# Attention backward: Z one iteration later, and eight blocks of E transposed in later iterations

## The chip, the cores and the metric

The kernel runs on one core of a Trainium2 chip. The metric is the device time of one execution in microseconds. A profiled execution gives, beside its time, a trace of all instructions: TensorE (PE, with its weight loads as PEld), VectorE (DVE), ScalarE (ACT), GpSimd (POOL) and SyncE (SP), which issues DMAs here.

## The reference

The reference is a layer with its gradients, in bfloat16: a layer norm, attention with 32 heads of width 16 over 2048 positions, multiplied by a gate that comes from a two-layer MLP, and a residual. What is asked for is the output and the gradients for the input and six weights. The part that this case is about is attention with its backward pass:

```
xn = layernorm(x)                       # x: 2048 x 512
q, k, v = split(xn @ wqkv)              # 32 heads of 16
p = softmax(q k^T * 16**-0.5)           # 2048 x 2048 for each head
s = (p v) @ wo
out = x + s * silu(mlp(xn))
# and the gradients of all this for x, wqkv, wo, w1, b1, w2, b2, given grad_out
```

For a head with probabilities p and the gradient dO of its output, the kernel needs sums over keys (the output O = p v, the row sums, and dQ) and sums over queries (dK and dV).

## The kernel before

The program has three stretches: a preparation (projections, the MLP's forward pass), the attention loop, and the remaining gradients. The loop is `attention_core`, and the change touches nothing else.

The loop works on pairs of heads (16 of them) and on quarters of the queries (512, `qc`), which makes 64 blocks `j`. In a block it steps over 16 units, `kb`, of 128 keys each. So there are 1024 units, and a unit's number `g` is also the number of the iteration that holds its main part. "Iteration 4" below means g % 16 = 4. "Key block 1" is the unit with kb = 1.

What is done for a unit:
- `emit_s` (L1115): two matmuls, one per head, give the scores s of 128 keys by 512 queries, in one PSUM tile of a pool with a single buffer. `emit_exp` (L1124, ACT) takes the exponential of both, E, into a ring of 11 SBUF tiles (`ets`).
- `emit_d` (L1137): two matmuls for d = v dO, each into one of three PSUM tiles. `emit_mult` (L1155, DVE) multiplies each with E; the product is G (`gts`). POOL copies one slot of E beside it (L1153).
- `emit_x` (L1232, L1235, L1239): three times four matmuls, which gather in PSUM tile X the sums over keys, from E, from E with ones, and from G. X is copied to SBUF by DVE (`emit_xs`, L1248) once a block, transposed by PE in two halves (`emit_XT`, L1266), copied back (`emit_xt`, L1274), and made into O, dQ and the weights W1 and W2 for Z by POOL (`emit_fin`).
- `emit_dmat` (L1172): a transposing DMA on SP's queue turns two units' G into `gk`.
- `emit_T` (L1192): PE transposes seven of the eight 128 by 128 pieces of E into the PSUM tile tT, of which there is one; the eighth piece is what POOL copied, and goes through the DMA. `emit_cT` (L1208, ACT) copies the result to the SBUF tile `ek`.

Z (`emit_z`, L1334) gathers the sums over queries in a PSUM tile, also single: four matmuls in each iteration, with W1 or W2 as weights and `gk` or `ek` as data. Eight iterations make one Z; then `emit_acc` (L1346 for the first quarter of queries, L1348 for the others, DVE) adds it to an SBUF sum. Z runs `ZOFF` iterations behind the units: at -20 the sums fall into iterations 11 and 3.

In units 0 and 5 the last 256 of the 512 columns of tT are needed for a transposed half of X (`FIN_AT`). For that, `cut` leaves out three of the seven transposes of these units, and ACT's copy is shorter by as much. The pieces left out are transposed later: the tile tT has room for eight pieces, and `OLDER` says in which unit the eighth place takes which older piece; (5, 1) is piece 1 of unit 5. DVE copies that place to `ek` (`emit_cO`, L1215), two iterations after the unit. Blocks from the second on do this; the first transposes all seven at once.

The order of the work is that of the emitted program: each engine goes through its own instructions in order and waits at each for what it needs. In an iteration g, PE's order is: first d of unit g, the two s of unit g+1, second d of unit g, four matmuls for Z, twelve for X of unit g-1, transposes of unit g-1 (and of X in iterations 1 and 6). In iteration 1 the G part of X is left out, and it is made up for in iteration 2, which has sixteen. DVE's order is: copy of the eighth place of unit g-2 if there is one, copy of a transposed half of X if there is one, first product of unit g, copy of X or sum of Z if there is one, second product. ACT's order is: exp of unit g+1, copy of T of unit g-1.

After the last unit the loop goes on for as many iterations as Z runs behind, in which `tail_mid` already starts the output projection (L584, with products by DVE at L586 and L591).

Of the kernel before, what the change touches and what calls it, by code (L numbers as in the profile page):

```python
# [1050 lines left out]
def attention_core(ctx, ctx_r, tc, k, grads, Oall, dQall, dKVT_out, ident_f32, ident_bf, npairs=16, nqc=4):  # L1051
# [67 lines left out]
    def emit_exp(g):  # L1119

        a = a_unit(g)
        if a is None:
            return
        nc.scalar.activation(out=st_et[g].rearrange("k b h q -> k h b q"),  # L1124
                             in_=cur["s"][:].rearrange("k h (b q) -> k h b q", b=4), func=ACT.Exp)
# [15 lines left out]
    def emit_mult(g):  # L1141
        a = a_unit(g)
        if a is None:
            emit_xs(g - 1)
            emit_acc(g + ZOFF)
            return
# [7 lines left out]
        for hj in range(2):  # L1154
# [3 lines left out]
            if hj == 0:  # L1158
                emit_xs(g - 1)
                emit_acc(g + ZOFF)  # L1160

# [9 lines left out]
            gk = blk[j]["Gk"][kc][:, kb % 4 - 1:kb % 4 + 1]  # L1171
            nc.sync.dma_start_transpose(out=gk.rearrange("q r x k -> q (r x) k"), in_=st_gt[g][:].rearrange("k a x q -> k (a x q)"))  # L1172

    OLDER = {4: (0, 0), 6: (0, 1), 7: (0, 2), 8: (5, 0), 12: (5, 1), 13: (5, 2)}

    def cut(g):
        return 3 if g >= 16 and g % 16 in (0, 5) else 0

    def older(g):
        return OLDER.get(g % 16) if 16 <= g < NSTEP else None  # L1180

    def emit_T(g):
        a = a_unit(g)
        if a is None:
            return
        kk = a[1] % 4
        et = st_et[g]
        t = ps_t.tile([128, 512], f32, name="tT")
        tb = t[:].bitcast(bf16).rearrange("q (i k) -> q i k", k=128)
        for i in range(cut(g), 7):  # L1190
            b = i + a[1] // 4 % 2
            nc.tensor.transpose(tb[:, i - cut(g), :], et[:, b // 2, b % 2, :], ident_bf[:])  # L1192
        if older(g):
            kk2, i = older(g)
            b = i + kk2 // 4 % 2
            nc.tensor.transpose(tb[:, 7, :], st_et[g // 16 * 16 + kk2][:, b // 2, b % 2, :], ident_bf[:])
        st_T[g] = t
        if kk == 0:
            cur["ek"] = ekc.tile([128, 4, 7, 128], bf16, name="ek")
            blk[a[0]]["Ek"][a[1] // 4] = cur["ek"]  # L1200

    def emit_cT(g):
        a = a_unit(g)
        if a is None:
            return
        j, kb = a
        c = cut(g)
        nc.scalar.copy(out=blk[j]["Ek"][kb // 4][:, kb % 4, c:7].rearrange("q i k -> q (i k)").bitcast(f32),  # L1208
                       in_=st_T[g][:, 0:(7 - c) * 64])
# [7 lines left out]
    def emit_x(g, part):  # L1217
        a = a_unit(g)
        if a is None:
            return  # L1220
        j, kb = a
        if part == "e" and kb == 0:
            blk[j]["X"] = ps_x.tile([128, 512], f32, name="X", tag="X")
        X = blk[j]["X"]
        NATt = op_of(j)["NAT"]
        et = st_et[g]
        for c in range(4):
            half, hj = c // 2, c % 2
            r = 32 * c
            ev = et[:, half::2, hj, :]  # L1230
            if part == "e":
                nc.tensor.matmul(X[r:r + 32, 0:256], lhsT=NATt[:, kb, hj, 1:33], rhs=ev,  # L1232
                                 start=(kb == 0), stop=False, skip_group_check=True, tile_position=(0, r))
            elif part == "l":
                nc.tensor.matmul(X[r:r + 32, 256:512], lhsT=Lc[:], rhs=ev,  # L1235
                                 start=False, stop=False, skip_group_check=True, tile_position=(0, r))
            else:
                gv = st_gt[g][:, kb % 2, 4 * hj + half:4 * hj + 4:2, :]
                nc.tensor.matmul(X[r:r + 17, 256:512], lhsT=NATt[:, kb, hj, 0:17], rhs=gv,  # L1239
                                 start=False, stop=(kb == 15), skip_group_check=True, tile_position=(0, r))  # L1240

    def emit_xs(g):
        a = a_unit(g)
        if a is None or a[1] != 15:
            return
        j = a[0]
        xs = xsp.tile([128, 512], f32, name="xs", tag="xs")
        nc.vector.tensor_copy(out=xs[:], in_=blk[j].pop("X")[:])  # L1248
        blk[j]["xs"] = xs
# [66 lines left out]
    def emit_z(g):  # L1316
        u = z_unit(g)
        if u is None:
            return
        j, kp, qb, part = u  # L1320
        if part == 0 and qb == 0:
            blk[j]["Z"] = ps_z.tile([128, 512], f32, name="Z", tag="z")
        Z = blk[j]["Z"]
        for par in range(2):
            kc = 2 * kp + par
            for hj in range(2):
                r = 64 * par + 32 * hj
                if part == 0:
                    mv = blk[j]["Gk"][kc][:, :, 4 * hj + qb, :]
                elif 2 * qb + hj == 7 * (1 - par):  # L1330
                    mv = blk[j]["Gk"][kc][:, :, 8, :]
                else:
                    mv = blk[j]["Ek"][kc][:, :, 2 * qb + hj - par, :]
                nc.tensor.matmul(Z[r:r + 32, :], lhsT=WT[j % 2][1 - part][:, qb, hj, :], rhs=mv,  # L1334
                                 start=(part == 0 and qb == 0), stop=(part == 1 and qb == 0), tile_position=(0, r))

    def emit_acc(g):
        u = z_unit(g)
        if u is None or u[2] != 0 or u[3] != 1:
            return  # L1340
        j, kp = u[0], u[1]
        p, qc = blocks[j]
        Z = blk[j]["Z"]
        av = acc[:, kp, :]
        if qc == 0:
            nc.vector.tensor_copy(out=av, in_=Z[:])  # L1346
        else:
            nc.vector.tensor_tensor(out=av, in0=Z[:], in1=av, op=ALU.add)  # L1348
        if qc == nqc - 1:
            ob = (outp.tile([128, 512], bf16, name="ob") if kp == 0 or j < NB - 1 else  # L1350
                  xsp.tile([128, 512], bf16, name="ob", tag="xs"))
            nc.gpsimd.tensor_copy(out=ob[:], in_=av)
            dv = dKVT_out[p * 64:(p + 1) * 64, :].rearrange("r (a b s) -> r a b s", a=2, b=2)
            for b in range(2):
                nc.gpsimd.dma_start(out=dv[:, kp, b, :], in_=ob[b * 64:(b + 1) * 64, :])

    FIN_AT = {1: 1, 6: 0}
    FIN_END = {1: 1, 2: 0}
    ZOFF = -20
    late = []  # L1360
    for hj in range(2):
        emit_s(0, hj)
    emit_exp(0)
    for g in range(NSTEP - ZOFF):
        cur["g"] = g
# [20 lines left out]
        emit_exp(g + 1)  # L1386
        emit_z(g + ZOFF)
        emit_x(g - 1, "e")
# [28 lines left out]
def full_kernel(ctx, tc, A_x, A_wqkv, A_wo, B_x, B_w1, B_b1, B_w2, B_b2, grad_out,  # L1417
# [35 lines left out]
    with ExitStack() as cO, tc.manual_schedule():  # L1453
        op0p = cO.enter_context(tc.tile_pool(name="op0", bufs=1, side="right", reuse_waits="tile"))
        k.op0 = make_op(nc, op0p, 0)
        k.Lc = op0p.tile([128, 32], bf16, name="Lc")
        nc.gpsimd.memset(k.Lc[:], 0.0)
        nc.gpsimd.memset(k.Lc[:, 17:18], 1.0)
        op0p.tile([128, 96], mybir.dt.uint8, name="pad_to_256r")
        kv, nat, q, do, natd = op_loads(k, k.op0, 0, nc.sync.dma_start)  # L1460
        first = dict(kv=kv, q=lambda: (nat(), q()), do=lambda g: (do(g * 512, g * 512 + 512), natd(g * 4, g * 4 + 4)))
        with ExitStack() as cP:
            Pre(cP, tc, k, first, A_x, A_wqkv, A_wo, B_w1, B_b1, B_w2, B_b2, grad_out)
        pO = cO.enter_context(tc.tile_pool(name="persistO", bufs=1, reuse_waits="tile"))
        k.Oall = pO.tile([128, NT, D], bf16, name="Oall", tag="Oall")
        k.dQall = pO.tile([128, NT, D], bf16, name="dQall", tag="dQall")
        grads = Grads(cO, tc, k, pO, op0p, A_x, grad_out, A_wqkv, A_wo, B_w1, B_w2,
                      (out_0, out_1, out_2, out_3, out_4, out_5, out_6, out_7))
        with ExitStack() as cB:
            attention_core(cB, cB.enter_context(ExitStack()), tc, k, grads, k.Oall, k.dQall, k.dKVT_s, k.ident_f, k.ident_bf)  # L1470
        grads.run()
# [56 lines left out]
```

## Time and profile before

| | |
|---|---|
| time, median of 3 runs | 2180.5 us (2179.21 to 2181.51) |
| profiled execution | 2180.46 us |
| its span, first to last instruction | 2178.8 us |
| granted TensorE clock, mean | 0.997 |
| first to last exp of the loop, start to start | 218.7 to 1837.4 us of the span |

The page gives busy times by engine over the whole span and groups of equal instructions, with the mean duration of one and the idle time of its engine ahead of them. Busy times of PE are those of pipelined matmuls, whose ends are modelled, so PE is at 98% without being at its peak. In the timeline each row is a run of equal instructions of one engine: start, duration of the run, engine, line, operation, names, shapes, count, and in brackets the idle time ahead of it with what ended it.

### The profile page before, as it was taken

Reading aid. Unit: us, or ns where it says so; the run is one execution under the profiler, and the core shown is the slowest. Engines: PE = TensorE matmul, PEld = TensorE weight load, DVE = VectorE, ACT = ScalarE, POOL = GpSimd, SP = SyncE. Lnnn points to the kernel's source line nnn. Section 1 sums busy time; section 2 is a strip of 40 time slices with the busy share of each in tenths; the row PEclk is TensorE's granted clock in tenths of the full one; section 3 lists DMA queues with packets and bytes.
Section 4 is the critical chain, followed back from the end, with each engine's and each line's share of the span. In section 5 each row is a group of like instructions: output and inputs, shape, how many; then the busy total and the mean of one; then the engine's idle time right before and its main releaser. Section 6 shows DMA issues by size and latency. Waiting matters only on the chain.

```text
span 2178.8 us, 74934 instructions
## 1 busy us (share of the span) xinstructions
PE 2133.0 (98%) x30659; PEld 1170.6 (54%) x30659; DVE 1898.0 (87%) x3523; ACT 1782.2 (82%) x2481; POOL 870.6 (40%) x2397
## 2 busy tenths in 40 slices
PE   6999999999999999999999999999999999899999
PEld 3444555555555555555555555555555555444444
DVE  6677899999999999999999999999999998788647
ACT  5664899999999999999999999999999997775224
POOL 4376434343434444343434344444434343511003
PEclk9999999999999999999999999999999999999999
DMA  7786999999999999999999999999999999999975
GB/s 235 248 281 202 205 199 198 209 195 200 208 204 198 209 201 201 202 200 206 203 199 201 202 203 201 204 203 204 200 202 206 194 213 212 294 251 240 246 209 178
DMA packets 1416569, 461.17 MB, mean 212 GB/s; under 512 B 1329118, under 2 KB 1400414, under 8 KB 1416224
## 3 DMA queue, kind: packets, MB, share of 16 engines
q1 hardware_dynamic: 1401920, 425.44, 100.3%
q0 software_dynamic: 12720, 29.37, 4.9%
q8 instruction: 240, 3.93, 0.8%
q10 hardware_dynamic: 1584, 1.57, 0.2%
q14 instruction: 105, 0.86, 0.1%
HBM read 62.79 MB, written 64.75 MB: 59 GB/s over the span
## 4 chain that ended last, share of the span: by engine, by line
PE 94%; DVE 2%; DMA 1%; ACT 1%; POOL 0%; issue 0%; SPq 0%; DVEq 0%; ACTq 0%; POOLq 0%
PE tT L1192 22%; PE Z L1334 15%; PE d L1137 15%; PE X L1239 6%; PE X L1232 5%; PE X L1235 5%; PE s L1115 3%; PE ps_dy L909 2%; PE ps_dw L742 2%; PE ps_dw L983 2%; PE ps_h L352 2%; PE ps_m L367 2%; PE ps_dh L875 2%; PE tT L1266 1%; PE ps_dxa L1027 1%; PE ps_dwkv L827 1%
## 5 line engine op out<-in xcount | busy, mean ns | idle before, releaser
L1155 DVE TENSOR_TENSOR gts<-d,ets 128x512 bf16<-128x512 f32 x2048 | 1302.2, 682 | 18.2 <-PE d L1137 3.9
L1124 ACT ACTIVATE ets<-s 128x1024 bf16<-128x1024 f32 x1024 | 1051.6, 1027 | 15.2 <-PE d L1137 3.9
L1208 ACT COPY ek<-tT 128x448 f32<-128x448 f32 (+1 forms) x1024 | 525.1, 513 | 115.0 <-PE tT L1192 31.3
L1192 PE MATMUL tT<-ident_bf,ets 128*128 128x128 bf16 x6790 | 557.9, 221 | 0.0
L1192 PEld LDWEIGHTS <-ets 128*128 128x128 bf16 x6790 | 382.5, 98 | 210.5 <-issue 195.2
L1137 PE MATMUL d<-QDT,KVT 32*128 32x512 bf16 x2048 | 469.4, 384 | 0.0
L1153 POOL COPY gts<-ets 128x128 bf16<-128x128 bf16 x1024 | 281.6, 297 | 387.5 <-ACT ets L1124 382.7
L1115 PE MATMUL s<-QDT,KVT 32*128 32x512 bf16 x2048 | 401.1, 379 | 2.4 <-ACT ets L1124 2.4
L1334 PE MATMUL Z<-gk,W 128*32 128x512 bf16 x2304 | 302.9, 389 | 1.4 <-DVE acc L1348 1.3
L1239 PE MATMUL X<-gts,NAT 128*17 128x256 bf16 x4096 | 290.6, 273 | 0.0
L1232 PE MATMUL X<-ets,NAT 128*32 128x256 bf16 x4096 | 290.4, 273 | 0.0
L1235 PE MATMUL X<-ets,Lc 128*32 128x256 bf16 x4096 | 290.3, 273 | 0.0
L1334 PEld LDWEIGHTS <-W 128*32 128x32 bf16 x4096 | 105.5, 93 | 238.2 <-issue 225.0
L1137 PEld LDWEIGHTS <-KVT 32*128 32x128 bf16 x2048 | 148.5, 91 | 114.3 <-issue 21.5
L1334 PE MATMUL Z<-ek,W 128*32 128x512 bf16 x1792 | 203.6, 389 | 0.0
L1235 PEld LDWEIGHTS <-Lc 128*32 128x32 bf16 x4096 | 110.1, 97 | 108.6
L1215 DVE COPY ek<-tT 128x64 f32<-128x64 f32 x378 | 84.9, 225 | 89.5 <-ACT ek L1208 76.0
L1404 POOL COPY tick<-gts 1x2 bf16<-1x2 bf16 x205 | 36.0, 175 | 313.5 <-DVE gts L1155 313.5
L1115 PEld LDWEIGHTS <-KVT 32*128 32x128 bf16 x2048 | 142.7, 91 | 12.3 <-issue 6.4
L1239 PEld LDWEIGHTS <-NAT 128*17 128x17 bf16 x4096 | 114.7, 91 | 15.4 <-issue 1.1
L1232 PEld LDWEIGHTS <-NAT 128*32 128x32 bf16 x4096 | 108.8, 96 | 5.1 <-issue 5.1
L1295 POOL TENSOR_TENSOR W<-NATQq,rL 128x128 bf16<-128x128 bf16 x64 | 25.5, 399 | 147.9 <-DVE rL L1294 110.3
(252 smaller groups left out, 2470.4 us busy)
## 6 DMA issues: line engine op xcount, KB each, us to landing
gk<-gts SPq DMA_TRANSPOSE x512, 5.6
H1T_s<-h1r SPq DMA_DIRECT2D x28, 256.0 KB, 4.2
HGT_s<-hgT SPq DMA_DIRECT2D x8, 896.0 KB, 4.5
DH_s<-stg SPq DMA_DIRECT2D x12, 512.0 KB, 3.3
hch<-DH_s SPq DMA_DIRECT2D x12, 512.0 KB, 4.8
gp<-H1T_s SPq DMA_DIRECT2D x9, 512.0 KB, 6.8
out_dram<-ob_w POOLq DMA_DIRECT2D x36, 128.0 KB, 4.6
NAT_s<-NS SPq DMA_DIRECT2D x4, 1056.0 KB, 6.1
```

Source lines behind the costliest of these rows:

```text
L1115: nc.tensor.matmul(s[:, hj, :], lhsT=op["KVT"][r:r + 32, kb * 128:(kb + 1) * 128], rhs=op["QDT"][r:r + 32, qc * 512:(qc + 1) * 512], start ...
L1124: nc.scalar.activation(out=st_et[g].rearrange("k b h q -> k h b q"), in_=cur["s"][:].rearrange("k h (b q) -> k h b q", b=4), func=ACT.Exp)
L1137: nc.tensor.matmul(d[:], lhsT=op["KVT"][r:r + 32, kb * 128:(kb + 1) * 128], rhs=op["QDT"][r:r + 32, qc * 512:(qc + 1) * 512], start=True, ...
L1153: nc.gpsimd.tensor_copy(out=gts[:, kb % 2, 8, :], in_=st_et[g][:, b // 2, b % 2, :])
L1155: nc.vector.tensor_tensor(out=gts[:, kb % 2, 4 * hj:4 * hj + 4, :], in0=st_d.pop((g, hj))[:].rearrange("k (b q) -> k b q", b=4), in1=st_et ...
L1192: nc.tensor.transpose(tb[:, i - cut(g), :], et[:, b // 2, b % 2, :], ident_bf[:])
L1208: nc.scalar.copy(out=blk[j]["Ek"][kb // 4][:, kb % 4, c:7].rearrange("q i k -> q (i k)").bitcast(f32), in_=st_T[g][:, 0:(7 - c) * 64])
L1215: nc.vector.tensor_copy(out=blk[g // 16]["Ek"][kk // 4][:, kk % 4, i].bitcast(f32), in_=st_T[g][:, 448:512])
L1232: nc.tensor.matmul(X[r:r + 32, 0:256], lhsT=NATt[:, kb, hj, 1:33], rhs=ev, start=(kb == 0), stop=False, skip_group_check=True, tile_positi ...
L1235: nc.tensor.matmul(X[r:r + 32, 256:512], lhsT=Lc[:], rhs=ev, start=False, stop=False, skip_group_check=True, tile_position=(0, r))
L1239: nc.tensor.matmul(X[r:r + 17, 256:512], lhsT=NATt[:, kb, hj, 0:17], rhs=gv, start=False, stop=(kb == 15), skip_group_check=True, tile_pos ...
L1334: nc.tensor.matmul(Z[r:r + 32, :], lhsT=WT[j % 2][1 - part][:, qb, hj, :], rhs=mv, start=(part == 0 and qb == 0), stop=(part == 1 and qb = ...
```

## The change

Two things are changed. `ZOFF` goes from -20 to -21: every matmul of Z and every sum is emitted one iteration later, the sums so in iterations 12 and 4, and the loop has one iteration more at its end. And `cut` now also leaves out the first two of the seven transposes of unit 1; ACT's copy of this unit gets 320 columns instead of 448. `OLDER` has eight entries instead of six: units 8 and 9 take pieces (1, 0) and (1, 1), unit 11 takes (5, 0), which unit 8 took before.

```
-    OLDER = {4: (0, 0), 6: (0, 1), 7: (0, 2), 8: (5, 0), 12: (5, 1), 13: (5, 2)}
+    OLDER = {4: (0, 0), 6: (0, 1), 7: (0, 2), 8: (1, 0), 9: (1, 1), 11: (5, 0), 12: (5, 1), 13: (5, 2)}

     def cut(g):
-        return 3 if g >= 16 and g % 16 in (0, 5) else 0
+        return {0: 3, 1: 2, 5: 3}.get(g % 16, 0) if g >= 16 else 0
...
     FIN_AT = {1: 1, 6: 0}
     FIN_END = {1: 1, 2: 0}
-    ZOFF = -20
+    ZOFF = -21
```

## The prediction

> **What bounds the kernel now.** I read the page's engine table first, then the groups of instructions with shapes kept apart, then the busy time of one block, then the timeline of that block row by row. A block is 16 iterations of the attention loop; there are 64 of them. I took the block that starts at 751.49 us, because the first rows (PE d L1137) of its iterations lie at the same distances as in most other blocks.
>
> ```profile
> PE 2133.0 (98%) x30659; PEld 1170.6 (54%) x30659; DVE 1898.0 (87%) x3523; ACT 1782.2 (82%) x2481; POOL 870.6 (40%) x2397
> ```
>
> ```profile
> L1155 DVE TENSOR_TENSOR gts<-d,ets 128x512 bf16<-128x512 f32 x2048 | 1302.2, 682 | 18.2 <-PE d L1137 3.9 <-ACT ets L1124 1.1 <-POOL tick L1404 1.0
> L1208 ACT COPY ek<-tT 128x448 f32<-128x448 f32 x898 | 478.2, 533 | 104.5 <-PE tT L1192 31.3 <-PE tT L1196 0.5
> L1215 DVE COPY ek<-tT 128x64 f32<-128x64 f32 x378 | 84.9, 225 | 89.5 <-ACT ek L1208 76.0
> L1208 ACT COPY ek<-tT 128x256 f32<-128x256 f32 x126 | 46.9, 372 | 10.5
> ```
>
> ```profile
> 751.49:776.71 25.22, 25.22 (x438) 14.40 (x437) 23.63 (x45) 23.32 (x33) 12.00 (x37) 1.00 1.26 208
> ```
>
> In this order the last row gives PE, PEld, DVE, ACT and POOL: in 25.22 us DVE is busy 23.63 and ACT 23.32, and the granted clock is 1.00. No engine has much to spare, so what counts is which of them ends last in each iteration. The timeline of iterations 2 to 6 shows it (start us, duration us; mergers of equal instructions have a count):
>
> ```profile
> 754.03 0.40 PE L1192 MATMUL tT<-ident_bf,ets 128*128 128x128 bf16 x4
> ...
> 755.18 1.02 ACT L1124 ACTIVATE ets<-s 128x1024 bf16<-128x1024 f32 x1
> ...
> 755.68 1.87 DVE L1155 TENSOR_TENSOR gts<-d,ets 128x512 bf16<-128x512 f32 x3
> 755.80 0.56 PE L1192 MATMUL tT<-ident_bf,ets 128*128 128x128 bf16 x7
> 756.30 0.39 PE L1137 MATMUL d<-QDT,KVT 32*128 32x512 bf16 x1
> ...
> 756.40 0.53 ACT L1208 COPY ek<-tT 128x448 f32<-128x448 f32 x1 [0.19 <-PE tT L1192]
> 756.41 0.37 PE L1137 MATMUL d<-QDT,KVT 32*128 32x512 bf16 x1
> 756.83 1.03 ACT L1124 ACTIVATE ets<-s 128x1024 bf16<-128x1024 f32 x1
> ...
> 757.47 0.68 DVE L1348 TENSOR_TENSOR acc<-Z,acc 128x512 f32<-128x512 f32 x1
> 757.87 0.38 PE L1137 MATMUL d<-QDT,KVT 32*128 32x512 bf16 x1
> 757.91 0.39 PE L1115 MATMUL s<-QDT,KVT 32*128 32x512 bf16 x2
> ...
> 757.97 0.53 ACT L1208 COPY ek<-tT 128x448 f32<-128x448 f32 x1
> 758.07 3.22 DVE L1155 TENSOR_TENSOR gts<-d,ets 128x512 bf16<-128x512 f32 x5
> 758.40 1.03 ACT L1124 ACTIVATE ets<-s 128x1024 bf16<-128x1024 f32 x1
> 758.68 0.40 PE L1239 MATMUL X<-gts,NAT 128*17 128x256 bf16 x4
> ...
> 759.51 0.38 PE L1137 MATMUL d<-QDT,KVT 32*128 32x512 bf16 x1
> 759.51 0.39 PE L1115 MATMUL s<-QDT,KVT 32*128 32x512 bf16 x2
> ...
> 760.28 0.28 PE L1239 MATMUL X<-gts,NAT 128*17 128x256 bf16 x4
> ...
> 761.05 0.39 PE L1137 MATMUL d<-QDT,KVT 32*128 32x512 bf16 x1
> ...
> 761.60 1.02 ACT L1124 ACTIVATE ets<-s 128x1024 bf16<-128x1024 f32 x1
> ```
>
> Iterations 3 to 6 begin at 756.30, 757.87, 759.51 and 761.05 with their first d. Four gates can be read off.
> (1) s has one PSUM tile, so it starts 0.05 after the exp before it ends (756.83 + 1.03 = 757.86, s at 757.91).
> (2) On ACT the copy of T stands between two exps: it starts 0.10 after PE's next d (757.87, 757.97), and the next exp 0.43 later (758.40), or 0.47 after s, whichever is last.
> (3) d has three tiles: the second d of iteration 3 waits for the first product of iteration 2. That began at 755.68, ended 0.68 later at 756.36, and d follows at 756.41 instead of beside the first d.
> (4) X's last group needs the second product of the unit before. With the sum of Z (757.47) in between, that product starts at 758.07 and ends at 758.75; the group of four, which elsewhere takes 0.28, takes 0.40: a stall of 0.12.
> One transpose costs PE (0.56 - 0.40) / 3 = 0.053, some 0.055 with rounding. From s to PE's next d it is 1.54 with eight transposes (759.51 to 761.05), so 1.48 with seven. On DVE a product or a sum sets back the next by 0.60 (757.47 to 758.07), 0.08 less than its 0.68; so a copy of 0.225 sets it back by 0.14.
>
> **The change, part by part.** PE has the same number of transposes: two leave unit 1 (iteration 2), an eighth appears for units 9 and 11 (iterations 10 and 12); unit 8 keeps its eighth, now another one. ACT's copy of unit 1 shrinks from 448 to 320 columns: between 372 and 533 ns, by columns 533 - 161 x 128/192 = 426, so 0.11 less. DVE gets 2 x 63 = 126 copies like L1215, in iterations 11 and 13. The sums go from iterations 3 and 11 to 4 and 12, every Z one iteration later. No DMA, POOL or SP instruction of the loop is moved past another; POOL's weights for Z get an iteration more.
>
> *Iterations 2 and 3.* T of unit 1 is 0.11 shorter, so the next d comes at 756.19. It gains PE nothing: gate 3 is DVE's, behind X's transposed copy, and its start at 755.68 does not depend on T. The second d stays at 756.41, and all PE work behind it, iteration 4 included (757.87), stays too. ACT gains: exp of unit 3 ends at 756.20, s at 756.25, exp of unit 4 at 756.72 instead of 756.83.
>
> *Iteration 4.* Without the sum, the second product of unit 3 starts at 757.47 and ends at 758.15, so the stall of 0.12 is gone; with s at 757.88 the next d comes at 757.88 + 1.48 = 759.36 instead of 759.51. But exp of unit 5 hangs on the copy at 757.97 and stays at 758.40.
>
> *Iteration 5.* s waits for that exp: 758.40 + 1.03 + 0.05 = 759.48, 0.03 earlier than now. DVE's first product of unit 4 can start at about 758.36 (0.38 for d and some 0.1 to start, as exp starts 0.08 behind an s of 0.39), the sum at 758.96, the second product at 759.56, ending at 760.24. X wants it at 759.48 + 0.77 = 760.25 (0.77 is 759.51 to 760.28) and needs 760.24 + 0.05: a stall of 0.04. The next d comes at 759.48 + 1.54 + 0.04 = 761.06, against 761.05. Exp of unit 7 then stands at 761.06 + 0.53 = 761.59, against 761.60. Both gains have been given back; about -0.01 to -0.02 goes on through iterations 6 to 9, which keep their instructions.
>
> *Iterations 10 to 13*, the same block:
>
> ```profile
> 768.88 0.38 PE L1137 MATMUL d<-QDT,KVT 32*128 32x512 bf16 x1
> 768.98 0.39 PE L1115 MATMUL s<-QDT,KVT 32*128 32x512 bf16 x2
> ...
> 768.99 0.53 ACT L1208 COPY ek<-tT 128x448 f32<-128x448 f32 x1
> 769.45 1.02 ACT L1124 ACTIVATE ets<-s 128x1024 bf16<-128x1024 f32 x1
> ...
> 770.01 0.68 DVE L1346 COPY acc<-Z 128x512 f32<-128x512 f32 x1
> 770.46 0.38 PE L1137 MATMUL d<-QDT,KVT 32*128 32x512 bf16 x1
> 770.53 0.39 PE L1115 MATMUL s<-QDT,KVT 32*128 32x512 bf16 x2
> ...
> 771.30 0.34 PE L1239 MATMUL X<-gts,NAT 128*17 128x256 bf16 x4
> ...
> 772.06 0.38 PE L1137 MATMUL d<-QDT,KVT 32*128 32x512 bf16 x1
> 772.08 0.39 PE L1115 MATMUL s<-QDT,KVT 32*128 32x512 bf16 x2
> ...
> 773.06 0.56 PE L1192 MATMUL tT<-ident_bf,ets 128*128 128x128 bf16 x7
> ```
>
> In iteration 11 s starts 0.10 after d: PE waits there for exp. The eighth transpose of iteration 10 moves d to 768.94 and hides in that wait; ACT's copy moves to 769.04 and the next exp to 769.47, 0.02 later. That is what remains of its 0.055. DVE's new copy waits, as the others do, until ACT's copy has ended (some 0.03 behind; gates 1 and 3 take 0.05): 769.04 + 0.53 + 0.03 = 769.60. With its 0.14 the products of iteration 11 start at 769.74 and 770.34, the latter ending at 771.02: the present stall of 0.06 in iteration 12 goes. It makes room for the eighth transpose there: s at 770.55, next d at 772.09 instead of 772.06. The sum now stands in iteration 12: first product 770.95, sum 771.55, second product 772.15 to 772.83. X in iteration 13 wants it at 772.10 + 0.77 = 772.87 and gets it at 772.88. The copy of iteration 13 starts at 772.19 + 0.56 = 772.75 and ends at 772.97; T, on the same PSUM tile, comes at 773.08, 0.06 after it may. So +0.03 at the end of iteration 13, less the 0.01 to 0.02 from the first half: +0.01 a block, with 0.03 either way for the rounding of the rows. Over 63 blocks: +0.6 us (-1.3 to +2.5).
>
> *The end of the loop.* One iteration more is emitted, and the last sums stand behind other work on DVE:
>
> ```profile
> 1845.99 0.68 DVE L1348 TENSOR_TENSOR acc<-Z,acc 128x512 f32<-128x512 f32 x1
> ...
> 1846.72 1.05 PE L1334 MATMUL Z<-gk,W 128*32 128x512 bf16 x16 [0.29 <-DVE acc L1348]
> ...
> 1847.18 0.68 DVE L591 TENSOR_TENSOR t<-ps_so,s1g 128x512 f32<-128x512 f32 x1
> ```
>
> Z waits for the sum, and the sum will now be queued behind the second pair of products of the output projection, whose last is the row at 1847.18. If these move up by the sum's 0.60, the sum starts at 1847.18 and Z at 1847.91, +1.2; if not, +1.8. I take +1.5. PE is the chain there, so it passes on; at the loop's start an iteration without Z more gains under 0.1.
>
> *The sum.* 2180.46 (the profiled execution: span 2178.8 and 1.66 around it; the median of the runs, 2180.5, is the same) + 0.6 + 1.5 = 2182.6 us.
>
> **A rule against this.** By matmul time PE is 98% busy, by weight loads 54%, DVE 87%. The Trainium skill, "Perfetto Trace Analysis", section "Identifying the Most-Contended Engine", holds matmul busy time for a bad measure of TensorE, takes weight loads instead, and calls the engine of highest occupancy the one to optimise first. By that rule DVE is the bound, and the change gives it more work. In rows: 126 copies x 0.14 = +17.8 us, which with the tail is 2199.8. Against it stands that DVE already waits for ACT before these copies (76.0 us at L1215).
>
> **The rivals.** *Faster, 2171:* gate 3 and ACT's copy in iteration 4 do not hold, and the gains reach the end: 0.11 + 0.12 + 0.06, less two transposes of 0.055, is 0.18 a block, -11.3 us, so 2170.7. For it speaks that both stalls are real; against it that 756.41 follows a DVE end by 0.05. It counts from 0.07 a block.
> *Slower, 2189, by transposes:* nothing covers the two added ones: 2 x 0.055 x 63 = +6.9, with the tail 2188.9. It decides if s in iteration 11 no longer waits for exp.
> *Slower, 2191, by the sum:* iteration 12 has only 0.01 to spare on DVE. If the copy's 0.14 before it is not absorbed, the second product, X and the copy of iteration 13 are late by 0.14: +8.8, with the tail 2191. It decides if the first product of unit 12 starts more than 0.07 later than 0.49 behind d.
> *Slower, 2200:* DVE as the bound, as above.
>
> **How the numbers follow.** Within 0.2% (4.4 us, about what a measurement tells from none): 0.52, its own range 2178 to 2186. Faster, 0.20. Slower by transposes 0.13, by the sum 0.12, by DVE as a whole 0.03: together 0.28. The range goes from 2174, more than half way to the faster rival, to 2190, which takes in the transposes and half of the sum's case.
>
> **What would show it.** After: the second d of iteration 3 some 0.2 behind the first (now 0.11); the group of four of X at 0.28 in iterations 4 and 12, near 0.32 in 5 and 0.29 in 13; 16 iterations in 25.2 us; 504 copies at L1215; the sum's wait in the tail near 1.7. Wrong would be a block under 25.15 or over 25.30, or a waiting X in iteration 13 of over 0.07.

## The result, and the profile after

| | before | after |
|---|---|---|
| time, median of 6 runs each | 2180.85 us (2177.54 to 2182.04) | 2194.14 us (2189.63 to 2198.32) |
| ratio of the times, 95% interval | | 1.0065 (1.005 to 1.008) |
| profiled execution | 2180.46 us | 2193.16 us |
| its span | 2178.8 us | 2191.4 us |
| preparation: start of the span to the first d | 218.1 us | 220.2 us |
| loop: first d to last d, start to start | 1620.4 us | 1632.9 us |
| rest: last d to the end | 340.3 us | 338.3 us |

The change makes the kernel slower by 0.65%, some 13 us. The predicted time was 2182.6 us and its range ended at 2190. The lower half of the table says where the difference of the two profiled executions (12.7 us) lies: 12.5 us are in the loop. The row from which the loop's end points come is that of d in the view by source line (durations in ns, then the first and the last start in us), here of the kernel after:

```profile
L1137 PE MATMUL d<-QDT,KVT x2048: 371/384/604, 220.2 to 1853.1; 32*128 32x512 bf16 x187
```

The engine table of the page, the groups with shapes kept apart, and the busy times of one block after the change (the block from 757.54, whose 16 iterations stand at the usual distances):

```profile
PE 2149.4 (98%) x30659; PEld 1172.8 (54%) x30659; DVE 1919.3 (88%) x3649; ACT 1783.0 (81%) x2481; POOL 865.4 (39%) x2397
```

```profile
L1155 DVE TENSOR_TENSOR gts<-d,ets 128x512 bf16<-128x512 f32 x2048 | 1312.7, 682 | 33.6 <-PE s L1115 18.5 <-PE d L1137 3.2 <-ACT ets L1124 1.2
...
L1215 DVE COPY ek<-tT 128x64 f32<-128x64 f32 x504 | 112.6, 223 | 69.9 <-ACT ek L1208 51.9
...
L1208 ACT COPY ek<-tT 128x320 f32<-128x320 f32 x63 | 26.8, 425 | 5.4 <-PE tT L1192 0.3
```

```profile
757.54:782.97 25.43, 25.43 (x439) 14.44 (x438) 23.91 (x47) 23.31 (x33) 11.92 (x37) 1.00 1.19 212
```

The change did what it says: 504 copies at L1215 instead of 378, and 63 copies on ACT of 320 columns, of 425 ns each. The granted clock is 1.00 in the block as before. The block takes 25.43 us instead of 25.22, with 0.28 more work on DVE. PE counts as busy for the whole block in both, but it runs no more matmuls than before (30659 in the program both times). One thing in the groups is new: DVE's products waited 18.5 us for PE, with "s" as the last to release them, where before 3.9 us for d led the list.

The lengths of the 16 iterations, from one first d to the next, are medians over 61 blocks, in ns (worked out from the starts of all first rows of d):

```
iteration    0    1    2    3    4    5    6    7    8    9   10   11   12   13   14   15    sum
before    1596 1497 1715 1570 1646 1538 1615 1550 1575 1576 1518 1576 1602 1556 1594 1504  25228
after     1553 1497 1604 1695 1482 1817 1538 1612 1553 1597 1553 1541 1609 1677 1537 1558  25423
```

Iterations 2 to 5 together are 0.129 longer and 10 to 13 are 0.128 longer; the other eight give back 0.062. That is +0.195 a block, and over 63 blocks 12.3 us: the loop's difference. Iteration 3 is 0.125 longer, of which iteration 2 gives back 0.111. The other two increases over 0.1, +0.279 in iteration 5 and +0.121 in iteration 13, are in the iterations that follow the two new sums. The timeline of the kernel after, iterations 3 to 5 (first d at 762.19, 763.89 and 765.37) and 12 and 13 (776.59 and 778.20):

```profile
762.19 0.38 PE L1137 MATMUL d<-QDT,KVT 32*128 32x512 bf16 x1
...
762.43 0.37 PE L1137 MATMUL d<-QDT,KVT 32*128 32x512 bf16 x1
...
763.89 0.38 PE L1137 MATMUL d<-QDT,KVT 32*128 32x512 bf16 x1
...
764.48 0.69 DVE L1155 TENSOR_TENSOR gts<-d,ets 128x512 bf16<-128x512 f32 x1 [0.31 <-PE s L1115]
764.66 0.28 PE L1239 MATMUL X<-gts,NAT 128*17 128x256 bf16 x4
765.09 0.68 DVE L1348 TENSOR_TENSOR acc<-Z,acc 128x512 f32<-128x512 f32 x1
765.37 0.39 PE L1137 MATMUL d<-QDT,KVT 32*128 32x512 bf16 x1
...
765.69 1.88 DVE L1155 TENSOR_TENSOR gts<-d,ets 128x512 bf16<-128x512 f32 x3
...
766.27 0.43 PE L1239 MATMUL X<-gts,NAT 128*17 128x256 bf16 x4
...
776.59 0.38 PE L1137 MATMUL d<-QDT,KVT 32*128 32x512 bf16 x1
...
777.43 0.28 PE L1239 MATMUL X<-gts,NAT 128*17 128x256 bf16 x4
777.77 0.68 DVE L1346 COPY acc<-Z 128x512 f32<-128x512 f32 x1
...
778.37 0.68 DVE L1155 TENSOR_TENSOR gts<-d,ets 128x512 bf16<-128x512 f32 x1
...
778.98 0.41 PE L1239 MATMUL X<-gts,NAT 128*17 128x256 bf16 x4
```

In iteration 4 the first product begins 0.59 behind d (763.89, 764.48), though DVE has stood idle for 0.31 and d ended at 764.27. The prediction had it 0.49 behind. Sum and second product follow at their usual distance of 0.60 (765.09, 765.69), so the second product ends at 766.37, and X's group of four takes 0.43 instead of 0.28. In iteration 13 it takes 0.41. These two waits are where the loss shows; the stalls of before, in iterations 4 and 12, are gone (0.28 each).

### The profile page after: what moved, and what is told of

It reads as the page before. It is cut to its first block, busy times and chain, and to the rows that moved or that the text cites. A ratio compares the mean times of both kernels' runs of the same rounds, so it can differ in the third digit from the quotient of the medians.

```text
span 2191.4 us, 75058 instructions
## 1 busy us (share of the span) xinstructions
PE 2149.4 (98%) x30659; PEld 1172.8 (54%) x30659; DVE 1919.3 (88%) x3649; ACT 1783.0 (81%) x2481; POOL 865.4 (39%) x2397
## 4 chain that ended last, share of the span: by engine, by line
PE 93%; DVE 2%; DMA 2%; ACT 1%; SPq 1%; POOL 0%; issue 0%; ACTq 0%; DVEq 0%; POOLq 0%
PE tT L1192 22%; PE d L1137 15%; PE Z L1334 15%; PE X L1239 6%; PE X L1232 5%; PE X L1235 5%; PE s L1115 3%; PE ps_dy L909 2%; PE ps_dw L983 2%; PE ps_h L352 2%; PE ps_dw L742 2%; PE ps_m L367 2%; PE ps_dh L875 2%; PE tT L1266 1%; PE tT L1196 1%; PE ps_dxa L1027 1%
## 5 line engine op out<-in xcount | busy, mean ns | idle before, releaser
L1155 DVE TENSOR_TENSOR gts<-d,ets 128x512 bf16<-128x512 f32 x2048 | 1312.7, 682 | 33.6 <-PE s L1115 18.5
L1208 ACT COPY ek<-tT 128x448 f32<-128x448 f32 (+2 forms) x1024 | 518.1, 506 | 123.1 <-PE tT L1196 31.3
L1192 PE MATMUL tT<-ident_bf,ets 128*128 128x128 bf16 x6664 | 550.7, 221 | 0.0
L1192 PEld LDWEIGHTS <-ets 128*128 128x128 bf16 x6664 | 375.3, 98 | 210.3 <-issue 195.0
L1137 PE MATMUL d<-QDT,KVT 32*128 32x512 bf16 x2048 | 476.6, 385 | 0.0
L1153 POOL COPY gts<-ets 128x128 bf16<-128x128 bf16 x1024 | 276.8, 295 | 373.6 <-ACT ets L1124 371.2
L1239 PE MATMUL X<-gts,NAT 128*17 128x256 bf16 x4096 | 295.9, 273 | 0.0
L1137 PEld LDWEIGHTS <-KVT 32*128 32x128 bf16 x2048 | 151.0, 90 | 114.4 <-issue 21.6
L1215 DVE COPY ek<-tT 128x64 f32<-128x64 f32 x504 | 112.6, 223 | 69.9 <-ACT ek L1208 51.9
L1115 PEld LDWEIGHTS <-KVT 32*128 32x128 bf16 x2048 | 144.9, 91 | 14.1 <-issue 5.2
L1196 PE MATMUL tT<-ident_bf,ets 128*128 128x128 bf16 x504 | 110.4, 219 | 0.0
```

The source lines that it names most:

```text
L1115: nc.tensor.matmul(s[:, hj, :], lhsT=op["KVT"][r:r + 32, kb * 128:(kb + 1) * 128], rhs=op["QDT"][r:r + 32, qc * 512:(qc + 1) * 512], start ...
L1137: nc.tensor.matmul(d[:], lhsT=op["KVT"][r:r + 32, kb * 128:(kb + 1) * 128], rhs=op["QDT"][r:r + 32, qc * 512:(qc + 1) * 512], start=True, ...
L1153: nc.gpsimd.tensor_copy(out=gts[:, kb % 2, 8, :], in_=st_et[g][:, b // 2, b % 2, :])
L1155: nc.vector.tensor_tensor(out=gts[:, kb % 2, 4 * hj:4 * hj + 4, :], in0=st_d.pop((g, hj))[:].rearrange("k (b q) -> k b q", b=4), in1=st_et ...
```

## The experiments

Two theories stood against each other after the result. *The start:* the first product of an even unit (4, 12) can't begin as soon behind d as that of an odd one, some 0.59 instead of 0.49; the sum, moved from odd iterations into even ones, passes this on to X. *The work:* DVE has become the bound in these stretches with the 126 copies, or the two added transposes on PE cost time.

### The two parts alone

The first kernel has the later Z and the table of before; the second has the new table and the earlier Z.

```
e1_z_alone:   after, with   OLDER and cut of before      (ZOFF = -21)
e2_t_alone:   after, with   ZOFF = -20                   (OLDER and cut of after)
```

> Z one iteration later alone, with the tables of before. Theory A (the first product of an even unit cannot start before 0.59 us behind its d, that of an odd unit at 0.49, so a sum of Z in iterations 4 and 12 makes the second product late): the whole loss is here, X in iterations 5 and 13 stalls by some 0.13 us each, a block is about 0.20 us longer than before, +12 us in all and +1.5 at the loop's end. Theory B (the loss comes from the two further transposes and copies): the sum harmless, -1 to +2 us.

> The tables of the change alone, Z and its sums where they were (iterations 3 and 11). Theory A: the copy by DVE in iteration 11 now stands ahead of the sum of that iteration, and the second product is late by the copy's wait: a block about 0.40 us longer, +25 us. Theory B: +7 to +12 us.

Measured: Z alone 2193.09 us, 1.005 (1.0034 to 1.0066) of the time before; the table alone 2201.69 us, 1.0088 (1.0068 to 1.0109). Their rows of d, in the order Z alone, table alone:

```profile
L1137 PE MATMUL d<-QDT,KVT x2048: 371/384/604, 219.2 to 1852.0; 32*128 32x512 bf16 x187
```

```profile
L1137 PE MATMUL d<-QDT,KVT x2048: 371/384/604, 218.0 to 1862.2; 32*128 32x512 bf16 x187
```

Z alone has a loop of 1632.7 us (1632.74 from the starts in ns), the whole change one of 1632.86. So with Z at -21 the table with its 126 copies, its two cut transposes and its two added ones costs nothing: a block takes 25425 ns without it and 25423 with it. With Z at -20 the same table costs 23.8 us (1644.1 against 1620.4), because in iteration 11 the new copy and the sum then stand ahead of one second product. The timeline of the table alone, iterations 11 and 12 (d at 776.42 and 777.95):

```profile
777.09 0.23 DVE L1215 COPY ek<-tT 128x64 f32<-128x64 f32 x1
...
777.24 0.68 DVE L1155 TENSOR_TENSOR gts<-d,ets 128x512 bf16<-128x512 f32 x1
777.83 0.68 DVE L1346 COPY acc<-Z 128x512 f32<-128x512 f32 x1
777.95 0.38 PE L1137 MATMUL d<-QDT,KVT 32*128 32x512 bf16 x1
...
778.43 1.88 DVE L1155 TENSOR_TENSOR gts<-d,ets 128x512 bf16<-128x512 f32 x3
...
778.57 0.40 PE L1334 MATMUL Z<-gk,W 128*32 128x512 bf16 x4
...
779.00 0.45 PE L1239 MATMUL X<-gts,NAT 128*17 128x256 bf16 x4
...
779.93 0.39 PE L1137 MATMUL d<-QDT,KVT 32*128 32x512 bf16 x1
```

Copy, product, sum, product: this order costs twice. The late sum ends only at 778.51, and the next matmuls for Z, which go into the PSUM tile that it reads, start just behind it at 778.57: 0.53 behind s by the medians, where it is 0.32 in iteration 11. Then X waits 0.17 for the late second product (0.45 against 0.28), and iteration 12 takes 1.98. So the copies can cost, but by where they stand and not by their sum. The loss of the whole change is that of the later Z.

### The sums in odd iterations again

```
e4_z22_old:      after, with   ZOFF = -22, OLDER and cut of before      (sums in iterations 5 and 13)
e10_z22_50at10:  the same, and in OLDER   8: (5, 0)  ->  10: (5, 0)
```

> Z two iterations later than before, with the tables of before: the sums fall into iterations 5 and 13, whose units are odd. Theory A: the first product starts 0.49 us behind d there, X does not stall, a block 0.05 us shorter than before, -3 us in the loop, up to +2 at its end. Theory C (a later Z is dear in itself, by its buffers being held longer): worse than Z one iteration later, over +12 us.

> Z two iterations later than before (sums in the odd iterations 5 and 13) with the tables of before, but the copy of piece (5, 0) of unit 10 instead of unit 8. Theory A: a block 0.06 us shorter than before, the loop -3.8 us, up to +2 at its end: 2177 to 2181 us.

Measured: 2178.95 us, 0.9991 (0.9976 to 1.0005), and 2179.56 us, 0.9998 (0.9987 to 1.0008). Neither differs from before, though both have one iteration more at the loop's end than the changed kernel. So a later Z is not dear in itself. A block takes 25183 and 25184 ns, 0.045 less than before. The timeline of the first, an even unit (12, d at 775.76) and the odd one after it (13, d at 777.32):

```profile
775.76 0.38 PE L1137 MATMUL d<-QDT,KVT 32*128 32x512 bf16 x1
...
776.34 1.29 DVE L1155 TENSOR_TENSOR gts<-d,ets 128x512 bf16<-128x512 f32 x2 [0.34 <-POOL gts L1153]
...
777.32 0.38 PE L1137 MATMUL d<-QDT,KVT 32*128 32x512 bf16 x1
...
777.81 0.69 DVE L1155 TENSOR_TENSOR gts<-d,ets 128x512 bf16<-128x512 f32 x1 [0.18 <-PE s L1115]
...
778.42 0.68 DVE L1346 COPY acc<-Z 128x512 f32<-128x512 f32 x1
```

DVE was idle ahead of both products. The even unit's begins 0.58 behind its d, the odd unit's 0.49. Over 60 blocks of this kernel the medians, in ns behind the first d, are:

```
unit                                    4     5    12    13
DVE free (end of the product before)  281   356   236   312
POOL's copy beside it ends            346   393   374  1666
d ends                                384   385   384   385
first product begins                  590   492   576   492
```

This is the cleanest comparison: one kernel, DVE free before d ends in all four units, and the same end of d. POOL's copy, which the trace names as releaser for unit 12, ends before d there, so it isn't what the product waited for.

### What the even unit waits with

An even unit's first product is DVE's first write into a new buffer of `gts` (there are four, each for two units; POOL's copy goes into another slot of it). The view by source line, in narrow windows, shows the instructions that DVE's sequencer ran for these products: units 4 and 5 of the block after, and unit 0 of the block before that the prediction used (751.49).

```profile
L1155 DVEq EVENT_SEMAPHORE  x2: 21/36/50, 764.3 to 764.4; - x2
...
L1155 DVEq EVENT_SEMAPHORE  x1: 21/21/21, 765.8 to 765.8; - x1
```

```profile
L1155 DVEq EVENT_SEMAPHORE  x2: 21/36/50, 751.9 to 752.0; - x2
```

Unit 4 has two such instructions, unit 5 has one. In unit 4 they start 0.43 and 0.50 behind d, and the second takes 0.05. The DMA that frees the buffer is not late for unit 4: in the kernel after it landed 0.7 to 5.7 us before the product, 3.2 by the median of 61 blocks (for unit 12 the trace holds no landing). The Trainium skill, "Perfetto Trace Analysis", section "Identifying Dependency Chains", says that an instruction waiting for several engines may get EventSemaphore instructions ahead of it with the further wait conditions. The trace agrees (two against one), and puts a price on it: 0.59 against 0.49.

The same rows of the kernel with Z at -22, as medians over 60 blocks in ns behind the first d, account for the whole 0.1:

```
unit                                    4          5        12          13
first wait instruction ends           447        447       433         448
second one runs                    495-545         -    481-531          -
first product begins                  590        492       576         492
```

In all four units the first product begins about 45 ns after the last wait instruction has ended. The second one, with the gap ahead of it, is the 98 ns by which unit 4 is later than unit 5. Opening a buffer doesn't always bring a second one: units 0, 4, 10, 12 and 14 have two, units 2, 6 and 8 have one.

To test it, a small write by DVE takes the buffer earlier, so that the first product of units 4 and 12 is no longer DVE's first write into it. In the first of the next kernels the write stands behind the second product of units 3 and 11, in the second behind those of 3 and 10:

```
e3_early_touch, after with
-        if kb % 2 == 0:
+        if kb % 2 == 0 and kb not in (4, 12):
             cur["gts"] = gtp.tile([128, 2, 9, 128], bf16, name="gts")
...
+        if kb in (3, 11):
+            cur["gts"] = gtp.tile([128, 2, 9, 128], bf16, name="gts")
+            nc.vector.memset(cur["gts"][0:1, 0, 0, 0:2], 0.0)

e8_touch, after with
-        if kb % 2 == 0:
+        if kb in (4, 12):
+            cur["gts"] = cur.pop("next")
+        elif kb % 2 == 0:
             cur["gts"] = gtp.tile([128, 2, 9, 128], bf16, name="gts")
...
+        if kb in (3, 10):
+            cur["next"] = gtp.tile([128, 2, 9, 128], bf16, name="gts")
+            nc.vector.memset(cur["next"][0:1, 0, 0, 0:2], 0.0)
```

> The changed kernel, in which the buffer of the products of units 4 and 12 is taken by a write of one element by DVE at the end of iterations 3 and 11, so that the first product itself no longer carries the waits for the buffer. Nothing else is left out. Theory A: the first product starts 0.49 us behind d in iterations 4 and 12, X in iterations 5 and 13 stalls by 0.04 us and less, and the loss goes: -10 us against the changed kernel, +1 to +3 against before. Theory B or any other: as the changed kernel, +13 us.

> As the experiment with the early write, but for unit 12 the buffer is taken at the end of iteration 10 instead of 11, so that the first product of unit 12 doesn't follow the write at once; for unit 4 at the end of iteration 3 as before. Theory A (the first product of an even unit starts late because of the waits that it carries for its buffer): first products at 0.48 behind d in iterations 4 and 12, X in iterations 5 and 13 at most 0.04 late, 16 iterations in 25.23 us, loop 12 us shorter than the changed kernel, so +1 to +3 us against before. If the lateness has another cause, such as DVE itself in iteration 12: half of that or nothing, +7 to +13 us.

Measured for the first: 2194.49 us, 1.0054 (1.0036 to 1.0072), a miss: no gain on the whole. By iterations it is half a hit. The first product of unit 4 starts at 0.479, and iteration 5 takes 1706 ns instead of 1817. But iteration 13 takes 1804 instead of 1677. The timeline of this kernel, iterations 11 to 13 (d at 773.90 and 775.51 for 12 and 13):

```profile
773.17 1.28 DVE L1155 TENSOR_TENSOR gts<-d,ets 128x512 bf16<-128x512 f32 x2
...
773.90 0.38 PE L1137 MATMUL d<-QDT,KVT 32*128 32x512 bf16 x1
...
774.39 0.06 DVE L1163 MEMSET gts<- 1x1 uint32 x1
774.61 0.69 DVE L1155 TENSOR_TENSOR gts<-d,ets 128x512 bf16<-128x512 f32 x1 [0.16 <-ACT ek L1211]
```

The second product of unit 11 ends late (774.45), behind the copy that now stands in iteration 11. The write comes behind it, and the first product of unit 12 waits for the write: it starts 0.16 after the write's end, and 0.71 behind d instead of 0.58. The row names a copy of ACT as releaser, but the product's wait instruction starts 0.06 after the write's end and the product 0.045 after that instruction's end, as in the two later kernels whose rows name DVE's write. The write itself had become the wait.

With the write for unit 12 moved to iteration 10, where DVE has room, the second kernel gives 2182.18 us, 1.002 (1.0004 to 1.0035). Its block, first the busy times, then the timeline of iteration 4 (d at 764.65) and of iterations 12 and 13 (the d of 13 at 778.85):

```profile
758.30:783.52 25.22, 25.22 (x438) 14.46 (x438) 23.75 (x49) 23.33 (x33) 11.97 (x37) 1.00 1.21 215
```

```profile
764.65 0.39 PE L1137 MATMUL d<-QDT,KVT 32*128 32x512 bf16 x1
764.88 0.06 DVE L1165 MEMSET gts<- 1x1 uint32 x1
...
765.13 0.69 DVE L1157 TENSOR_TENSOR gts<-d,ets 128x512 bf16<-128x512 f32 x1 [0.20 <-PE s L1115]
...
767.03 0.32 PE L1244 MATMUL X<-gts,NAT 128*17 128x256 bf16 x4
...
778.85 0.39 PE L1137 MATMUL d<-QDT,KVT 32*128 32x512 bf16 x1
...
779.63 0.31 PE L1244 MATMUL X<-gts,NAT 128*17 128x256 bf16 x4
```

The view by source line, for the first product of unit 4 in this kernel:

```profile
L1157 DVEq EVENT_SEMAPHORE  x1: 92/92/92, 765.0 to 765.0; - x1
```

Only one wait instruction is left there; it ends 0.434 behind d by the median, and the product again begins 0.044 later.

Both first products now start 0.48 behind d (medians 478 in units 4 and 12), X's groups in iterations 5 and 13 take 0.32 and 0.31 (the prediction had 0.32 and 0.29), and the block is back at 25.22 us (25216 by the medians). Two writes of 0.06 have taken away what the change cost in a block: 25423 - 25216 = 207 ns, by 63 blocks 13.0 us. The profiled loops are 7.3 us apart (1632.86 and 1625.55), and the second holds one pause of 5.7 us in a single block, which together is 13.0 too. By the medians the whole change but for this one wait is then neutral in a block (25216 against 25228 ns), as the prediction had it. The kernel's time stays 0.2% above before; in the profiled execution the loop is 5.2 us longer, which the pause covers.

### The writes in the kernel before

A control: the same two writes in the kernel before, where the sums stand in odd iterations and no gain is to be had.

> The control: the same early writes in the kernel before. There the first products of units 4 and 12 follow right behind a late second product and don't wait for their buffer. Theory A: no gain, 0 us; the writes cost at most 0.06 us x 128 on DVE, where they lie beside other waits, so up to +2 us. If the writes help or harm by themselves: a block as much shorter or longer here as in the changed kernel, -12 us.

Measured: 2186.32 us, 1.0034 (1.0021 to 1.0047): no gain, as expected, but a loss that was not. The timeline, iterations 3 to 5 (d at 758.28, 759.85 and 761.50):

```profile
759.85 0.38 PE L1137 MATMUL d<-QDT,KVT 32*128 32x512 bf16 x1
...
760.05 0.68 DVE L1157 TENSOR_TENSOR gts<-d,ets 128x512 bf16<-128x512 f32 x1
...
760.68 0.06 DVE L1165 MEMSET gts<- 1x1 uint32 x1
...
760.89 2.48 DVE L1157 TENSOR_TENSOR gts<-d,ets 128x512 bf16<-128x512 f32 x4 [0.16 <-DVE gts L1165]
```

Here the sum is in iteration 3 and its second product is late (760.05), so the write is too, and the first product of unit 4 waits for the write until 1.04 behind d, where it is at 0.80 without it. Iteration 5 takes 1649 ns instead of 1538, of which later iterations give back some: the block is at 25291, 63 ns longer, 4.0 us over 63 blocks (its loop is 1625.6 us, +5.2). It is the same mechanism as in the first kernel with writes: such a write is free only where DVE has time to spare behind it.

### A version meant to be faster

The changed kernel with the writes of the second kernel above, but with one transpose cut from unit 1 instead of two, and the older pieces placed where the prediction's rules, stepped through all 16 iterations with 0.48 for these starts, gave the shortest block:

```
-    OLDER = {4: (0, 0), 6: (0, 1), 7: (0, 2), 8: (1, 0), 9: (1, 1), 11: (5, 0), 12: (5, 1), 13: (5, 2)}
+    OLDER = {1: (0, 0), 3: (0, 1), 6: (0, 2), 7: (1, 0), 11: (5, 0), 12: (5, 1), 13: (5, 2)}
-        return {0: 3, 1: 2, 5: 3}.get(g % 16, 0) if g >= 16 else 0
+        return {0: 3, 1: 1, 5: 3}.get(g % 16, 0) if g >= 16 else 0
```

> Z as in the changed kernel, with the early writes, one transpose of unit 1 left out instead of two, and the copies of older pieces in units 1, 3, 6, 7, 11, 12 and 13: none in the iterations just before the sums with the write. Theory A, by the four gates: a block 0.09 us shorter than before, the loop -5.5 us, +1.5 at its end: about 2177 us. A copy in iteration 3 or 5 that blocks a gate not seen so far would give over 2181.

Measured: 2191.41 us, 1.0045 (1.0029 to 1.0061), a miss by 14 us. The timeline around the write in iteration 3 (d of iteration 4 at 759.70):

```profile
759.70 0.39 PE L1137 MATMUL d<-QDT,KVT 32*128 32x512 bf16 x1
...
760.11 0.06 DVE L1165 MEMSET gts<- 1x1 uint32 x1
760.32 0.69 DVE L1157 TENSOR_TENSOR gts<-d,ets 128x512 bf16<-128x512 f32 x1 [0.16 <-DVE gts L1165]
```

The copy of unit 1's eighth place, in iteration 3, makes DVE late; the write ends at 760.17, and the product, 0.16 later, starts 0.62 behind d. Iteration 5 takes 1721 ns. The rules had no wait for the write in them. That is only a part of the miss. By the medians the block takes 25263 ns, 35 more than before where 90 less were expected, 7.9 us over 63 blocks; which other steps of the rules failed was not worked out. The profiled loop, 9.7 us longer than before, also holds five waits of 0.9 to 3.7 us, 7.7 together, in which such a write stood until the DMA that frees its buffer had landed: the early write asks for the buffer sooner. No kernel of the study is measurably faster than the one before.

## Why the prediction was wrong

*The gates and iterations 2 to 4: right.* The second d of iteration 3 stands 0.24 behind the first (762.43 and 762.19; predicted 0.2). Iteration 2 is shorter by 0.111 and iteration 3 longer by 0.125: the two cut transposes gain PE nothing, because d waits for DVE's product (gate 3). Iteration 4 takes 1.482 (predicted 1.49), and the stall of its X group is gone.

*Iteration 5: the failed term.* It is in this sentence of the prediction: "DVE's first product of unit 4 can start at about 758.36 (0.38 for d and some 0.1 to start". That is 0.49 behind d. Measured is 0.589, because a second wait instruction stands behind the wait for d. Iteration 5 takes 1.82 where the prediction had 1.70 (759.36 to 761.06); with the writes, which bring the start to 0.478, it takes 1.705. The 0.1 came from an ACT instruction, and the rows of before bear it out only for odd units: unit 5 begins 0.491 behind d, unit 13 too. The first products of units 4 and 12 stood later in before (0.796 and 0.751), behind a late second product, so their own rows do not show what they need by themselves. The rows of DVE's sequencer do, in the kernel before as well: in unit 4 the second wait instruction ends 0.544 behind d, in unit 5 the only one ends at 0.446 (medians over 60 blocks). The row of unit 0 (two EVENT_SEMAPHORE, product at 752.08, 0.588 behind d) was the hint, though there the product of unit 15 ends only at that moment.

*Iterations 10 to 13: the same term again.* The eighth transpose of iteration 10 and the copy of iteration 11 are hidden as worked out: X takes 0.28 in iteration 12. The "first product 770.95" of the prediction is 0.49 behind d; measured is 0.575. X waits 0.13 in iteration 13 (0.41 against 0.28) where the prediction had 0.01, and said that over 0.07 would make it wrong. The block, 25.42, is also beyond the 25.30 that it named.

*The sum, with the term set right.* 0.10 more in iteration 4 and 0.09 more in iteration 12, both passed on in full, are 0.19 on top of the predicted 0.01: 0.20 a block, 12.6 us over 63 blocks, where the loop shows 12.5. That it fits so closely is in part luck. The kernel with the second pair of writes, whose starts are at 0.48, shows what each stretch does without the late starts: against it, iterations 2 to 5 of the changed kernel are 0.128 longer, 10 to 13 0.100 longer, and the other eight 0.021 shorter. And against before, that kernel's iterations 2 to 5 are 0.001 and 10 to 13 0.028 longer, near the prediction's -0.01 to -0.02 and +0.03, but its other eight are 0.040 shorter, which the prediction didn't have. So the gates and the order held in the stretches that were worked out, and the step that failed is one start latency, used twice and taken 0.09 to 0.10 too small. The rival "by the sum" named the place and the point at which it decides (over 0.07 later than 0.49 behind d, in unit 12), but with another cause, the copy ahead of it, and for one of the two sums only; it gave 2191 and had a chance of 0.12.

*The tail: right in its place, not seen in the time.* Z's wait for the last sum went from 0.29 to 1.43 (the prediction had it near 1.7), and Z starts 1.42 later behind the last d (9.64 against 8.22; predicted +1.5). After:

```profile
1862.04 0.68 DVE L1348 TENSOR_TENSOR acc<-Z,acc 128x512 f32<-128x512 f32 x1
...
1862.78 1.05 PE L1334 MATMUL Z<-gk,W 128*32 128x512 bf16 x16 [1.43 <-DVE acc L1348]
```

Still the rest of the program took 2.0 us less than before, and the preparation, which has the same instructions, 2.1 more. In the other kernels with this Z the rest took 336.3 to 342.1 us: a scatter in which 1.5 is lost.

*The rivals.* "By transposes": not so, the table costs nothing with this Z. "DVE as the bound", with the rule of the Trainium skill, "Perfetto Trace Analysis", section "Identifying the Most-Contended Engine", behind it: the trace differs. DVE has the highest share after matmuls (88%), and 126 more copies on it, with the rest of the new table, left the loop at 1632.86 us against 1632.74. With Z at -20 the same table cost 23.8 us, but by where its copies stand. "Faster": what the two stalls of before give is real (0.28 for X in iterations 4 and 12), but it was gone by iteration 5 as worked out.

*What stays open.* That DVE's first write into the buffer is what makes units 4 and 12 late is shown by the kernels with writes (0.48 against 0.59 and 0.58), and the wait instructions account for the time between. Whether the second one would cost nothing if it stood ahead of the wait for d was not tested.

Four of the kernels (both with Z at -22, the one with writes that is back at 25.22, and the version meant to be faster) show in their profiled loops one pause each of 3.6 to 5.7 us, in one block only; the block lengths above are medians and leave it out. By the trace each is a wait for a transposing DMA that frees a buffer of `gts`: the write that opens it, or the first product, stood idle for 2.1 to 3.7 us until then. In the kernel with writes that is back at 25.22:

```profile
521.01 0.06 DVE L1165 MEMSET gts<- 1x1 uint32 x1 [3.44 <-DMA gk<-gts]
```

All four come behind a load of 264 KB (`NAT`) that POOL issues once in a pair of heads. There it took 8.8 to 9.7 us from issue to landing; in all its other uses in the ten traces it took 3.2 to 8.4, the 8.4 with a wait of 1.2 us for a buffer behind it. Why the load was slow in these four is not shown.

## What to carry to other kernels

Where gates decide, a start latency is a term of the sum like a duration: take it from the same kind of instruction in the same role. Here an engine's first write into a recycled buffer was another role than the second, and the wait instructions that the trace shows ahead of a product told the two apart. When a step is moved by one iteration, ask which property alternates between iterations (here, the unit that opens a buffer) and whether the step has left one side for the other. A small early write can take such a wait off a critical instruction, but only where its engine is ahead; behind a late instruction it is itself the next wait.

## What the runs showed of the hardware that was not expected

- With Z at -22, a DVE product that waits for PE and has two wait instructions ahead of it starts 0.19 to 0.21 behind the end of d (0.590 and 0.576 against 0.384 in units 4 and 12), one with a single wait instruction 0.11 (0.492 against 0.385 in units 5 and 13).
- A DVE product that waits for a DVE write just ahead of it starts 0.15 to 0.16 after that write's end (760.17 to 760.32), though otherwise a product begins some 0.08 before the end of the one before it (764.48 + 0.69 = 765.17, the sum at 765.09).
